# A sparse causal attention and a gated layer on one core: the sign mask of the queries taken from PSUM by halves, the relu moved to GpSimd, and a new written order

## The chip, the core and the metric

One core of a Trainium2 chip. The metric is the time of one execution on the device in microseconds; lower is better. The kernel before takes 178.91 us (median of 3 runs, 178.85 to 181.53).

## What is computed

Four batches, eight heads, 768 positions, head dimension 64. The keys are cut into 24 chunks of 32. For each query an upper bound of its score with any key of a chunk is computed from the chunk's minimum and maximum; the six best causal chunks are kept, and softmax attention runs over these alone. A gated layer follows.

```python
k_min, k_max = k_chunks.min(axis=3), k_chunks.max(axis=3)
ub = sum over d of maximum(q * k_min, q * k_max)
ub = where(causal, ub, -1e9); top_chunks = argsort(ub)[..., -6:]
scores = where(selected and causal, q @ k.T / 8, -1e9)
x = softmax(scores) @ v                       # heads side by side: 768 x 512
gate = sigmoid(causal convolution over 5 positions of x, per channel)
out = (gate * (x @ w_val)) @ w_out
```

Since max(q*min, q*max) = relu(q)*(max - min) + q*min, the bound is a matrix product of relu(q) and of q with two small key matrices. As the choice of six chunks needs more than fp16 gives, queries and keys are split into a high part and a low rest, both fp16: QH and QL of the queries, and for their positive part RH and RL.

## The kernel before

The work is done by pairs of heads: 16 pairs, four to a batch. All of a pair's steps are named in `build` with the pair's number behind the name:

- `Lk`, `Lq`, `Lv` load keys, queries and values (SP's queue). `KT` and `QT` turn keys and queries on TensorE into two PSUM banks each (L663), one for the head in either half (0 and 1).
- `KE` (L677, ScalarE) copies the turned keys to fp16. `KX` (L688, VectorE) takes maximum and minimum of each chunk; `KB` and `KS` (L696 to L713, GpSimd) make the small key matrices KB from them.
- `QH` (L717, ScalarE) writes the high part of the queries from PSUM, a half at a time. `QL` (L757, VectorE) takes the low rest, again from PSUM by halves. `RH` (L764, VectorE) is the maximum of QH and zero, `RM` (L770, VectorE) is QH > 0 as 0 or 1; each is one operation over 640 columns that reads and writes fp16 in SBUF. `RL` (L776, GpSimd) is QL times RM. Pair 0 does the same in fp32 (`KF`, `QF`, `RF`, `BF`).
- `CF` and `BD` (L743, L802, TensorE) add up the bounds from RH, RL, QH and QL with KB; `T8` (L810, VectorE) finds the eight largest and `CM` (L817) marks the chunks below the sixth. The marks are turned into a mask QM by TensorE and VectorE (`MT`, `ME`, L831) or by a DMA (`MD`).
- `S` (L845 to L850, TensorE) are six scores a pair, each for two heads, with the penalty added by a second product with the constant EM; `E` (L854, ScalarE) takes the exponentials; `A` (L866, GpSimd) sets the part above the diagonal to zero; `VC` (L786, GpSimd) casts the values; `AV` (L875, TensorE) multiplies; `RC` and `NR` (L881, L895, VectorE) divide by the sums.
- Per batch: the convolution for two of the pairs as products with diagonal matrices (`CV`, L950; the matrices `dg`, L1122, GpSimd) and for the other two as `CA` (L958) and four `CD` each (L963, VectorE); `TH` (tanh, ScalarE), `VL` (L976, L981, TensorE), `GV` (L986, VectorE), `OU` (L994, TensorE), `OE` (L1002 ScalarE, L1004 VectorE) and the store `ST`. The weights are loaded through GpSimd's queue (`wval`, `wnat`, `wout`).

Every operation of every engine stands in one long list of names, `ORDER`, written out in the file. `emit_in_order` issues the operations exactly in that order and gives PSUM banks (eight) out as the list comes to them, so that the list sets the order on each engine's queue and who gets which bank when. A bank is free again once the last operation that reads it has been issued; the next writer waits for that reader on the chip. The costs in `build` are those of the program that once made the list, and are not used when the kernel is built. RH, RL and RM have two buffers each, for even and odd pairs. `F` and `G` are 48 products with zeros that occupy TensorE during the start.

Of the kernel before, what the change touches and what calls it, by code (L numbers as in the profile page):

```python
# [1164 lines left out]
```

## Time and profile before

| | |
|---|---|
| median of 3 runs | 178.91 us (178.85 to 181.53) |
| profiled execution, its own time | 181.09 us |
| its span, first to last instruction | 179.3 us |
| busy: TensorE, VectorE, ScalarE, GpSimd | 167.9, 151.4, 151.3, 109.4 us |
| granted TensorE clock | 0.999 |
| data moved by DMA | 28.76 MB |

The profile is one execution. Busy time of TensorE is the union of its products, which overlap; a waiting engine shows as idle time in front of an instruction, with the instruction that released it behind an arrow. Row names are the tile written, the tiles read and the line. A row of the stretches gives the start and end of a stretch, its length, and the busy time of PE (TensorE), PEld (its weight loads), DVE (VectorE), ACT (ScalarE) and POOL (GpSimd) in it.

### The profile page before, as it was taken

To read this page: it belongs to the slowest core of one execution; us is meant where nothing else is said; L and a number is where in the kernel's file an instruction comes from. 1 tells how busy PE (TensorE), PEld (TensorE's weight loads), DVE (VectorE), ACT (ScalarE), POOL (GpSimd) and SP (SyncE) were. 2 spreads that over 40 slices of the span, in tenths; PEclk is the share of its full clock that TensorE was granted. 3 is DMA by queue.
4 is the path that set the end of the run, shared out by engine and by line. 5 is a ranking of instruction groups with operands and counts; after the bars stand their busy time and mean duration, and the time that the engine had idled before them with its cause. 6 is when DMAs were issued, how large, how long until landed. Compare 5 with 4: busy or idle time off the path is not lost.

```text
span 179.3 us, 7859 instructions
## 1 busy us (share of the span) xinstructions
PE 167.9 (94%) x3214; PEld 113.6 (63%) x3214; DVE 151.4 (84%) x456; ACT 151.3 (84%) x328; POOL 109.4 (61%) x231
## 2 busy tenths in 40 slices
PE   7999789999999999999999999977999999999991
PEld 5787557675676856667756587454855756685540
DVE  0599989984999999999999999986797899569960
ACT  3378899999999999799999998957699999979241
POOL 5758788999797998158829349687228913610000
PEclk9999999999999999999999999999999999999999
DMA  4999989984993999805990556927295370240955
GB/s 92 240 266 207 256 201 252 214 197 93 214 208 53 206 196 239 191 4 119 294 232 8 110 113 97 277 51 126 38 251 164 65 149 0 47 179 4 346 217 197
DMA packets 87315, 28.76 MB, mean 160 GB/s; under 512 B 82923, under 2 KB 84203, under 8 KB 87280
## 3 DMA queue, kind: packets, MB, share of 16 engines
q1 hardware_dynamic: 86192, 27.21, 63.2%
q0 software_dynamic: 1088, 1.06, 3.9%
q8 instruction: 25, 0.41, 1.0%
q14 instruction: 10, 0.08, 0.2%
HBM read 20.98 MB, written 6.29 MB: 152 GB/s over the span
## 4 chain that ended last, share of the span: by engine, by line
PE 60%; ACT 14%; DVE 10%; DMA 5%; POOL 5%; issue 4%; SPq 1%; ACTq 0%; POOLq 0%; DVEq 0%
PE ps L994 8%; ACT P L854 8%; PE ps L875 8%; PE ps L847 7%; PE ps L981 6%; PE ps L850 5%; PE ps L976 5%; PE ps L950 4%; PE ps L663 4%; PE ps L802 4%; DMA wn<-in_moe_w_val_dram 3%; DVE KK L688 3%; DVE QL L757 2%; ACT QH L717 2%; PE ps L1012 2%
## 5 line engine op out<-in xcount | busy, mean ns | idle before, releaser
L854 ACT ACTIVATE P<-ps 128x512 f16<-128x512 f32 (+1 forms) x192 | 91.5, 581 | 5.8 <-PE ps L875 2.7
L850 PE MATMUL ps<-QM,EM 64*128 64x512 f16 (+4 forms) x256 | 37.6, 290 | 0.7 <-DVE QM L831 0.7
L847 PE MATMUL ps<-QH,KE 64*128 64x512 f16 (+4 forms) x256 | 35.7, 292 | 1.7 <-DVE QL L757 1.6
L688 DVE TENSOR_REDUCE KK<-ps 128x12 f32<-128x384 f32 x64 | 32.0, 545 | 5.8 <-PE ps L655 4.8
L866 POOL TENSOR_SCALAR_AFFINE_SELECT P<-P 128x256 f16<-128x256 f16 (+1 forms) x64 | 32.6, 529 | 5.5 <-ACT P L854 3.8
L963 DVE SCALAR_TENSOR_TENSOR G<-ps,cwT,G 128x764 f32<-128x764 f16 (+3 forms) x32 | 32.1, 1006 | 2.6 <-ACT G L958 2.3
L776 POOL TENSOR_TENSOR RL<-QL,RM 128x640 f16<-128x640 f16 x15 | 21.1, 1409 | 12.1 <-DVE RM L770 10.9
L875 PE MATMUL ps<-VA,P 128*128 128x65 f16 x672 | 27.8, 194 | 0.1
L875 PEld LDWEIGHTS <-P 128*128 128x128 f16 x672 | 24.0, 98 | 4.9 <-issue 2.1
L994 PE MATMUL ps<-wo,GV 128*128 128x512 f16 (+1 forms) x100 | 22.7, 371 | 0.0
L847 PEld LDWEIGHTS <-KE 64*128 64x128 f16 x256 | 13.8, 94 | 9.5 <-issue 2.5
L677 ACT ACTIVATE KE<-ps 128x384 f16<-128x384 f32 x32 | 15.7, 537 | 4.5 <-PE ps L655 2.9
L895 DVE TENSOR_TENSOR ON<-ps,RCP 128x384 f16<-128x384 f32 x32 | 17.3, 552 | 0.6
L786 POOL CAST VA<-vn 128x768 f16<-128x768 f32 x16 | 13.8, 865 | 6.5 <-DMA vn<-in_v_dram 6.3
L757 DVE SCALAR_TENSOR_TENSOR QL<-ps,QH 128x320 f16<-128x320 f32 x30 | 14.0, 483 | 4.1 <-ACT QH L717 3.3
L986 DVE SCALAR_TENSOR_TENSOR GV<-G,ps 128x384 f16<-128x384 f32 x32 | 16.0, 547 | 1.4 <-PE ps L981 0.9
L810 DVE MAX8 TOP<-ps 128x8 f32<-128x12 f32 (+4 forms) x160 | 15.9, 163 | 1.2 <-PE ps L802 1.0
L1002 ACT ACTIVATE OSB<-ps 128x512 f32<-128x512 f32 (+1 forms) x22 | 13.3, 626 | 4.0 <-PE ps L994 4.0
L717 ACT ACTIVATE QH<-ps 128x384 f16<-128x384 f32 x32 | 14.9, 519 | 1.3 <-PE ps L663 1.2
L994 PEld LDWEIGHTS <-GV 128*128 128x128 f16 x100 | 9.0, 97 | 9.2 <-issue 0.6
L850 PEld LDWEIGHTS <-EM 64*128 64x128 f16 x256 | 12.4, 95 | 3.0 <-issue 1.7
L802 PE MATMUL ps<-KB,RH 128*128 128x48 f16 x150 | 13.0, 184 | 1.3 <-DVE TOP L810 1.0
(88 smaller groups left out, 328.9 us busy)
## 6 DMA issues: line engine op xcount, KB each, us to landing
vn<-in_v_dram SPq DMA_DIRECT2D x16, 384.0 KB, 5.1
out_dram<-OSB SPq DMA_DIRECT2D x23, 256.0 KB, 2.6
kn<-in_k_dram SPq DMA_DIRECT2D x30, 192.0 KB, 3.8
qn<-in_q_dram SPq DMA_DIRECT2D x30, 192.0 KB, 4.1
wo<-in_moe_w_out_dram POOLq DMA_DIRECT2D x4, 128.0 KB, 4.8
kn<-in_k_dram SPq DMA_DIRECT2D x4, 96.0 KB, 2.6
qn<-in_q_dram SPq DMA_DIRECT2D x4, 96.0 KB, 2.8
wv<-in_moe_w_val_dram POOLq DMA_DIRECT2D x4, 64.0 KB, 3.3
```

The costliest lines, as they stand in the source:

```text
L688: nc.vector.tensor_reduce(out=o, in_=i, axis=AX.X, op=ALU.min if mx else ALU.max)
L717: nc.scalar.activation(out=spread(QH[p % 3], p, w), in_=bank(gr, None), func=AF.Copy, scale=QS)
L757: nc.vector.scalar_tensor_tensor(out=spread(QL[p % 2], p, w), in0=bank(gr, None)[:, 1:NT], scalar=QS, in1=spread(QH[p % 3], p, w)[:, 1:NT] ...
L776: nc.gpsimd.tensor_tensor(out=RL[p % 2], in0=QL[p % 2], in1=RM[p % 2], op=ALU.mult)
L802: nc.tensor.matmul(out=o, lhsT=lt, rhs=kb[:, j, :], start=False, stop=(n == 5), skip_group_check=True)
L847: nc.tensor.matmul(out=pq[hh][:, col + a:col + n], lhsT=KE[p % 3][HP[hh], ks], rhs=QH[p % 3][HP[hh], q0 + a:q0 + n], start=True, stop=False)
L850: nc.tensor.matmul(out=pq[hh][:, col + a:col + n], lhsT=EM[HP[hh], ks], rhs=qm[HP[hh], q0 + a - 128:q0 + n - 128], start=False, stop=True)
L854: e.EX = lambda p, hh, bi, tot, gr: nc.scalar.activation(out=PT[bi, p % 2][:, hh, 0:tot], in_=bank(gr, None)[:, 0:tot], func=AF.Exp, scale ...
L866: nc.gpsimd.affine_select(out=ap, in_=ap, pattern=[[0, 2], [0, n], [1, 128]], compare_op=ALU.is_ge, fill=0.0, base=0, channel_multiplier=-1)
L875: nc.tensor.matmul(out=pav[:, qt, :], lhsT=PT[bi, p % 2][:, a, col:col + 128], rhs=VA[p % 3][:, hh, jt, :], start=(jt == 0), stop=(jt == qt))
L963: nc.vector.scalar_tensor_tensor(out=GT[sl][:, d:S], in0=bank(gr, None)[:, 0:S - d], scalar=cwT[:, NG + p % 2, n:n + 1], in1=GT[sl][:, d:S ...
L994: nc.tensor.matmul(out=po[:, 0:z - a], lhsT=GVT[(b % 2) * NCT + et][:, s * 128:(s + 1) * 128], rhs=wout_sb[:, et, a:z], start=(et == 0), s ...
```

## The change

Three things. RM is taken from the fp32 queries in PSUM instead of from QH in SBUF, by halves (two operations of 128x320 a pair instead of one of 128x640), like QL. RH is no longer a maximum on VectorE but the product of QH and RM on GpSimd, like RL. And the list of names is another one.

```diff
@@ build, queries
             n = SELT * 64
             c, l = dve(n)
-            if w:
-                g.op("DVE", 231, 320, f"RH{p}", lambda: e.RHv(p), [("QH", k3, w) for w in range(2)],
-                     [("RH", k2, w) for w in range(2)], ())
+            g.op("DVE", c, l, f"RM{p}.{w}", lambda w=w, gr=gr: e.RMv(p, w, gr), [("qps", p, w)],
+                 [("RM", k2, w)], [gr])
             g.op("DVE", c, l, f"QL{p}.{w}", lambda w=w, gr=gr: e.QLv(p, w, gr),
                  [("qps", p, w), ("QH", k3, w)], [("QL", k2, w)], [gr])
             if w:
-                g.op("DVE", 231, 320, f"RM{p}", lambda: e.RMv(p), [("QH", k3, w) for w in range(2)],
-                     [("RM", k2)], ())
+                g.op("POOL", 1350, 1396, f"RH{p}", lambda: e.RHv(p),
+                     [("RM", k2, w) for w in range(2)] + [("QH", k3, w) for w in range(2)],
+                     [("RH", k2, w) for w in range(2)], ())
                 g.op("POOL", 1350, 1396, f"RL{p}", lambda: e.RLv(p),
-                     [("RM", k2)] + [("QL", k2, w) for w in range(2)],
+                     [(x, k2, w) for x in ("RM", "QL") for w in range(2)],
                      [("RL", k2, w) for w in range(2)], ())
...
     def RHv(p):
-        nc.vector.tensor_scalar(out=RH[p % 2], in0=QH[p % 3][:, 128:S], scalar1=0.0, scalar2=None,
-                                op0=ALU.max)
+        nc.gpsimd.tensor_tensor(out=RH[p % 2], in0=QH[p % 3][:, 128:S], in1=RM[p % 2], op=ALU.mult)
-    def RMv(p):
-        nc.vector.tensor_scalar(out=RM[p % 2], in0=QH[p % 3][:, 128:S], scalar1=0.0, scalar2=None,
-                                op0=ALU.is_gt)
+    def RMv(p, w, gr):
+        nc.vector.tensor_scalar(out=spread(RM[p % 2], p, w), in0=bank(gr, None)[:, 1:NT],
+                                scalar1=0.0, scalar2=None, op0=ALU.is_gt)
```

The first and the last names of the list, before and after:

```diff
-mfz cwl F0 F1 F2 F3 F4 F5 Lk0.1 F6 F7 F8 F9 F10 F11 F12 mNS0 F13 F14 ident F15 KT0.1 cwn0 cwn1
-identb aw Lk0.0 KT0.0 mKB1 identh KE0.1
+Lk0.0 mfz cwl ident identh Lk0.1 Lk2.0 mKF0 F0 mNS1 F1 F2 F3 F4 F5 F6 F7 F8 aw mVA1 F9 F10 F11 F12
+F13 F14 F15 KT0.0 KX0.00 KX0.01 KT0.1 KX0.11 KE0.1 KX0.10
...
-OU3.2 OE3.2 ST3.2 OU3.1 OE3.1 ST3.1 OU3.0 OE3.0 ST3.0 OU3.5 OE3.5 ST3.5
+ST3.5z ST3.1 OU3.0 OE3.0 ST3.0 OU3.2 OE3.2 ST3.2
```

Three places of the new order. In the rows, ps is a PSUM tile; a buffer's number is that of its place in the ring (RM_107 belongs to even pairs, RM_108 to odd ones). Lines of the new kernel stand one or two higher.

*First*, VectorE right after QM of pair 0, with the first scores ahead. Before:

```order
L831 COPY QM_91<-ps_395 128x640
L757 SCALAR_TENSOR_TENSOR QL_102<-ps_403,QH_99 128x5x64
L770 TENSOR_SCALAR RM_108<-QH_99 128x640
L757 SCALAR_TENSOR_TENSOR QL_102<-ps_404,QH_99 128x5x64
L764 TENSOR_SCALAR RH_104<-QH_99 128x640
L764 TENSOR_SCALAR RH_103<-QH_100 128x640
L688 TENSOR_REDUCE KK_112<-ps_461 128x6x2
L688 TENSOR_REDUCE KK_112<-ps_460 128x6x2
L770 TENSOR_SCALAR RM_107<-QH_100 128x640
```

and after:

```order
L832 COPY QM_91<-ps_397 128x640
L759 SCALAR_TENSOR_TENSOR QL_102<-ps_358,QH_99 128x5x64
L759 SCALAR_TENSOR_TENSOR QL_102<-ps_359,QH_99 128x5x64
L771 TENSOR_SCALAR RM_107<-ps_403 128x5x64
L771 TENSOR_SCALAR RM_107<-ps_404 128x5x64
L759 SCALAR_TENSOR_TENSOR QL_101<-ps_403,QH_100 128x5x64
L759 SCALAR_TENSOR_TENSOR QL_101<-ps_404,QH_100 128x5x64
L690 TENSOR_REDUCE KK_112<-ps_465 128x6x2
```

The two relus are gone from here, and RM and QL of pair 2 stand in four halves ahead of the key maxima of pair 3; RM of pair 1 has moved ahead of QM, where QL of pair 2 stood.

*Second*, VectorE around the queries of pairs 12 to 14, with the key maxima of pair 14 between them. Before:

```order
L770 TENSOR_SCALAR RM_108<-QH_99 128x640
L688 TENSOR_REDUCE KK_111<-ps_3380 128x6x2
L688 TENSOR_REDUCE KK_111<-ps_3379 128x6x2
...
L764 TENSOR_SCALAR RH_103<-QH_98 128x640
L764 TENSOR_SCALAR RH_104<-QH_99 128x640
...
L810 MAX TOP_119<-ps_3429 128x8 x10
L817 TENSOR_TENSOR NS_121<-ps_3429,TOP_119 128x10x24
L764 TENSOR_SCALAR RH_103<-QH_100 128x640
L757 SCALAR_TENSOR_TENSOR QL_101<-ps_3641,QH_100 128x5x64
```

and after:

```order
L771 TENSOR_SCALAR RM_108<-ps_3368 128x5x64
L771 TENSOR_SCALAR RM_108<-ps_3369 128x5x64
...
L690 TENSOR_REDUCE KK_111<-ps_3414 128x6x2
L690 TENSOR_REDUCE KK_111<-ps_3413 128x6x2
...
L811 MAX TOP_119<-ps_3455 128x8 x10
L818 TENSOR_TENSOR NS_121<-ps_3455,TOP_119 128x10x24
L771 TENSOR_SCALAR RM_107<-ps_3442 128x5x64
L771 TENSOR_SCALAR RM_107<-ps_3441 128x5x64
L759 SCALAR_TENSOR_TENSOR QL_101<-ps_3441,QH_100 128x5x64
L759 SCALAR_TENSOR_TENSOR QL_101<-ps_3442,QH_100 128x5x64
```

The three relus have left the queue; two RM halves stand ahead of each pair's QL.

*Third*, GpSimd from the last load of `wval` to the key matrix of pair 7. Before:

```order
L1085 DMA wv_66<-in_moe_w_val_dram 32x2x512
L866 AFFINE_SELECT P_0_124<-P_0_124 128x4x128
L866 AFFINE_SELECT P_0_127<-P_0_127 128x2x128
L776 TENSOR_TENSOR RL_106<-QL_102,RM_108 128x640
L700 TENSOR_SCALAR KC_116<-KK_112 128x48
L713 TENSOR_TENSOR KC_116<-KQ_114,KC_116 128x48
L708 COPY KB_118<-KC_116 64x4x24 x2
```

and after:

```order
L1086 DMA wv_66<-in_moe_w_val_dram 32x2x512
L777 TENSOR_TENSOR RL_105<-QL_101,RM_107 128x640
L766 TENSOR_TENSOR RH_103<-QH_98,RM_107 128x640
L867 AFFINE_SELECT P_0_126<-P_0_126 128x2x256
L867 AFFINE_SELECT P_1_132<-P_1_132 128x2x256
L1092 DMA wn_67<-in_moe_w_val_dram 128x512
L713 TENSOR_SCALAR KQ_114<-KK_112 128x48
L766 TENSOR_TENSOR RH_104<-QH_99,RM_108 128x640
L702 TENSOR_SCALAR KC_116<-KK_112 128x48
L715 TENSOR_TENSOR KC_116<-KQ_114,KC_116 128x48
L710 COPY KB_118<-KC_116 64x4x24 x2
L777 TENSOR_TENSOR RL_106<-QL_102,RM_108 128x640
```

Four products over 640 columns, RL and RH of pairs 6 and 7, now stand between these two points, where one stood, the RL of pair 7.

More of the change, by code (lines that the diff above doesn't have):

```diff
@@ L205 @@
[L205 to L207 removed]
+Lk0.0 mfz cwl ident identh Lk0.1 Lk2.0 mKF0 F0 mNS1 F1 F2 F3 F4 F5 F6 F7 F8 aw mVA1 F9 F10 F11 F12
+F13 F14 F15 KT0.0 KX0.00 KX0.01 KT0.1 KX0.11 KE0.1 KX0.10 G0 mKB1 G1 G2 cwn1 KE0.0 identb KF0.01
+KF0.00 cwn0 cwt cws G3 G4 G5 G6 G7 KT2 KE2.1 KF0.10 KF0.11 KX2.11 KX2.01 G8 G9 G10 G11 G12 cfill
@@ new lines @@
+VC6 AV6.01 E7.12 Lq13.0 A6.4 AV6.02 AV6.12 T88.1 AV6.03 AV6.11 QH10.0 KE10.0 OE0.2 T88.4 T88.5
+T88.3 AV6.13 CM8 MT8 AV6.10 OU0.0 KE10.1 RM10.0 AV6.14 ME8 OE0.1 QL10.0 KX10.11 KX10.10 OE0.0
+AV6.15 S8.5 Lv10 E8.15 RC6.1 NR6.1 S8.1 E8.11 AV6.05 E8.05 AV6.00 AV6.04 RC6.0 E8.01 XT4 XTE4 S8.3
+E8.03 RH9 E8.13 KB9.0 NR6.0 KT11 S8.0 E8.00 S8.4 E8.04 E8.14 KB9.1 KS9 KX11.01 KB9.2 KB9.3 KX11.11
+CF9 KX11.00 RL9 KB9.4 BD9.1 BD9.4 BD9.3 KX11.10 BD9.2 BD9.5 E8.10 S8.2 KE11.1 QT11 A7.3 VC7 A7.1
+RL10 AV7.11 A7.4 AV7.14 T89.3 AV7.13 QH11.1 T89.2 AV7.04 AV7.12 T89.5 AV7.10 T89.4 T89.1 CM9 MT9
@@ new lines @@
+AV9.01 E10.04 AV9.02 E10.00 KX13.10 AV9.05 RC9.0 VL1.3 KX13.11 NR9.0 QT12 RM12.1 KE13.1 VL1.3z
+GV1.30 GV1.31 QH12.0 MD11 S11.5 QH12.1 RM12.0 E11.05 S11.3 E11.03 AV9.13 AV9.15 E11.15 RH12 QL12.1
+AV9.14 AV9.11 E11.13 QL12.0 Lv15 RL12 AV9.10 AV9.12 RC9.1 S11.1 E11.01 A10.1 S11.0 E11.10 KB12.2
+XT8 KB12.3 NR9.1 QT13 RM13.0 E11.11 VL1.2 RM13.1 KB13.0 S11.4 QH13.0 QL13.0 VL1.2z QH13.1 QL13.1
+E11.00 XT9 GV1.21 KT14 KX14.11 KX14.01 KB12.4 E11.14 E11.04 S11.2 E11.02 KX14.10 GV1.20 QT14 CF12
+KE14.0 KX14.00 E11.12 BD12.1 BD12.2 BD12.3 BD12.5 BD12.4 KE14.1 T812.3 QH14.1 OU1.5 OE1.5 T812.1
@@ new lines @@
+T812.4 T812.5 T812.2 CM12 XH9 CV9.0 A10.3 RL13 A11.4 CV9.1 TH9.00 TH9.11 A11.3 TH9.01 OU1.0 OE1.0
+TH9.10 A10.4 OU1.1 OE1.1 ST0.0 MD12 S12.5 S12.4 RM14.1 RM14.0 ST1.5 QH14.0 QL14.0 AV10.05 Lv12
+E12.05 AV10.04 QL14.1 AV10.03 AV10.02 E12.04 AV10.15 E12.15 AV10.13 AV10.10 AV10.11 AV10.12 AV10.14
+E12.14 Lq15.0 AV10.01 KB14.0 AV10.00 RC10.1 S12.1 E12.11 A11.1 KT15 RC10.0 NR10.0 NR10.1 S12.0
+E12.01 S12.2 S12.3 Lv14 KS13 KB13.1 KX15.01 KX15.10 E12.10 KX15.11 KB13.2 KB13.4 E12.00 E12.03 CF13
+RH13 KE15.1 KB13.3 BD13.1 BD13.4 BD13.3 A12.5 BD13.2 BD13.5 E12.02 XT10 KX15.00 T813.3 T813.1
@@ new lines @@
+AV11.01 T813.5 T813.4 AV11.04 AV11.02 AV11.00 KS14 AV11.03 CA10 A11.5 AV11.05 T813.2 CM13 QT15
+QH15.1 KB14.1 RC11.0 NR11.0 KB14.2 KB14.3 KB14.4 CD10.0 KE15.0 E12.13 QH15.0 OU1.2 OE1.2 RL14 A12.4
+QL15.1 OU1.4 ST1.1 OE1.4 CF14 RH14 BD14.3 BD14.2 E12.12 BD14.1 BD14.5 CD10.1 XTE10 MD13 RM15.1
+AV11.15 AV11.12 AV11.13 AV11.10 AV11.14 AV11.11 RC11.1 NR11.1 BD14.4 S13.4 E13.04 QL15.0 S13.1
+E13.01 E13.11 RM15.0 OU1.3 OE1.3 T814.4 T814.1 A12.1 VC12 T814.3 T814.2 T814.5 CM14 A12.3 AV12.03
+AV12.04 XT11 RL15 XTE11 E13.14 S13.3 CD10.2 E13.13 E13.03 ST0.5 CA11 CD10.3 VL2.0 VL2.0z GV2.01
@@ new lines @@
+AV12.13 AV12.00 AV12.05 AV12.02 AV12.01 RC12.0 GV2.00 ST1.0 AV12.10 AV12.14 AV12.15 S13.5 E13.15
+E13.05 NR12.0 S13.0 E13.00 E13.10 MD14 CD11.0 S14.2 S14.5 E14.05 AV12.11 AV12.12 RC12.1 KB15.0
+KB15.1 CF15 KS15 KB15.2 KB15.3 NR12.1 KB15.4 RH15 BD15.3 BD15.2 BD15.5 BD15.4 A13.5 A13.3 BD15.1
+S13.2 T815.1 E14.12 E14.15 VL2.1 VC15 Lv13 VC13 E14.02 S14.1 T815.5 T815.2 T815.4 T815.3 CM15 MD15
+E13.12 VL2.1z A14.5 CD11.1 A13.1 S14.4 E13.02 E14.11 S14.0 GV2.10 E14.01 VC14 GV2.11 E14.04 E14.14
+A14.4 VL2.2 S14.3 ST1.2 E14.10 VL2.2z CD11.2 CD11.3 E14.00 A13.4 AV13.14 AV13.02 TH10 AV13.15
@@ L238 @@
 PX = True
+RV = 2
 NPAIR = B * H // 2
```

161 lines of the change are left out of this document (65 added, 96 removed).

## The prediction

> **What bounds the kernel now.** I read the page's totals first, then the busy time by stretches, then single instructions of the two lines that change, then TensorE's own gaps.
>
> ```profile
> PE 167.9 (94%) x3214; PEld 113.6 (63%) x3214; DVE 151.4 (84%) x456; ACT 151.3 (84%) x328; POOL 109.4 (61%) x231
> ```
>
> TensorE is busy 94% of the span. The stretches say where the others stand beside it (start and end, length, then busy us of PE, PEld, DVE, ACT and POOL). Their borders are the first scores of pairs 0, 3, 6, 10, 13 and 15, found in the timeline by the 64x128 product that each pair has once, in the score listed first or nearly so.
>
> ```profile
> 0.00:16.00 16.00, 14.59 (x140) 11.62 (x141) 9.57 (x36) 8.38 (x21) 10.69 (x31) 1.00 0.93 209
> 16.00:37.20 21.20, 19.34 (x392) 13.95 (x393) 19.58 (x77) 20.32 (x48) 17.89 (x36) 1.00 0.99 224
> 37.20:63.00 25.80, 24.69 (x610) 17.53 (x608) 22.47 (x76) 25.24 (x59) 22.80 (x47) 1.00 0.73 157
> 63.00:105.60 42.60, 42.18 (x844) 27.98 (x845) 41.70 (x119) 40.38 (x86) 26.15 (x56) 1.00 0.72 157
> 105.60:130.70 25.10, 22.68 (x534) 15.78 (x534) 21.38 (x70) 19.98 (x48) 17.08 (x36) 1.00 0.54 114
> 130.70:151.90 21.20, 20.96 (x330) 12.69 (x330) 18.95 (x52) 20.65 (x43) 11.42 (x21) 1.00 0.52 124
> 151.90:170.00 18.10, 18.10 (x355) 11.36 (x355) 14.09 (x26) 13.60 (x26) 3.43 (x8) 1.00 0.39 135
> 170.00:179.30 9.30, 5.38 (x29) 2.64 (x27) 3.66 (x7) 2.77 (x5) 0.00 (x0) 0.98 0.59 215
> ```
>
> No single engine bounds it all. From 63 to 105.6 VectorE is busy 98% and TensorE 99%; from 37.2 to 63 ScalarE 98%, with GpSimd at 88%. TensorE idles 1.86, 1.11, 0.42, 2.42 and 0.24 us in the five stretches from 16.0 to 151.9, 6.05 us in all: that is what a better order can win there. GpSimd has room only after 63.
>
> **What the changed lines cost now.** First the groups (busy total, mean ns), then minimum, median and maximum of the same two lines.
>
> ```profile
> L764 DVE TENSOR_SCALAR RH<-QH 128x640 f16<-128x640 f16 x15 | 9.0, 613 | 2.5 <-ACT QH L717 2.5
> L770 DVE TENSOR_SCALAR RM<-QH 128x640 f16<-128x640 f16 x15 | 6.5, 434 | 0.0
> L764 DVE TENSOR_SCALAR RH<-QH x15: 301/321/1977, 17.3 to 141.7; 128x640 f16<-128x640 f16 x15
> L770 DVE TENSOR_SCALAR RM<-QH x15: 286/319/1117, 16.6 to 139.0; 128x640 f16<-128x640 f16 x15
> ```
>
> Median and mean lie far apart: most take 0.32 us, a few take up to 1.98. By the medians they would sum to 15 x 0.321 + 15 x 0.319 = 9.6 us; they sum to 15.5. Some 5.9 us are spent in a few long ones. The timeline shows what runs beside those:
>
> ```profile
> 17.32 1.74 DVE L764 TENSOR_SCALAR RH<-QH 128x640 f16<-128x640 f16 x2
> 17.48 1.40 POOL L776 TENSOR_TENSOR RL<-QL,RM 128x640 f16<-128x640 f16 x1
> 116.61 1.99 DVE L764 TENSOR_SCALAR RH<-QH 128x640 f16<-128x640 f16 x2
> 117.03 1.39 POOL L776 TENSOR_TENSOR RL<-QL,RM 128x640 f16<-128x640 f16 x1
> 122.85 1.98 DVE L764 TENSOR_SCALAR RH<-QH 128x640 f16<-128x640 f16 x1 [2.53 <-ACT QH L717]
> 122.86 1.01 POOL L866 TENSOR_SCALAR_AFFINE_SELECT P<-P 128x256 f16<-128x256 f16 x2
> 123.83 0.82 POOL L786 CAST VA<-vn 128x768 f16<-128x768 f32 x1
> 124.75 0.48 DVE L757 SCALAR_TENSOR_TENSOR QL<-ps,QH 128x320 f16<-128x320 f32 x1
> ```
>
> Each long one ends when a run of GpSimd's work ends: at 122.85 the relu sits out two masks and a cast (until 124.65), and QL starts at 124.75. So these SBUF-to-SBUF forms wait for GpSimd, while QL, which reads PSUM, never took over 0.49 us in 30 times:
>
> ```profile
> L757 DVE SCALAR_TENSOR_TENSOR QL<-ps,QH x30: 462/482/492, 14.7 to 138.6; 128x320 f16<-128x320 f32 x30
> ```
>
> The Trainium skill states this in SBUF — State Buffer, Who interferes with whom: a copy or tensor_scalar that uses both SBUF ports of VectorE, and a GpSimd instruction, hold a shared port pair one at a time and for their whole length, whereas one with at most one SBUF input outside those modes does not compete. The trace agrees (1.98 us against a median of 0.321; QL's maximum 0.492).
>
> Do the long ones reach TensorE? Its three largest inner gaps:
>
> ```profile
> 21.09 0.21 PE L802 MATMUL ps<-KB,RH 128*128 128x48 f16 x2 [1.02 <-DVE TOP L810]
> 119.12 1.20 PE L950 MATMUL ps<-xT,diag 32*32 32x384 f16 x82 [0.94 <-DVE KK L688]
> 125.28 0.39 PE L847 MATMUL ps<-QH,KE 64*128 64x512 f16 x1 [1.14 <-DVE QL L757]
> ```
>
> Each comes shortly after one of the three long stalls and is released by what stands behind it on VectorE: 1.02 + 0.94 + 1.14 = 3.1 us.
>
> **The change part by part.** *1. The stalls go.* The compare now reads PSUM, like QL, and the relu leaves VectorE. At the three places I count VectorE's own time. A half-size operation out of PSUM is priced at 0.42 us (part 2). Around 17.32 (first pair of order fences) six of them now stand where two QL halves, two RM and the two relus stood: 2.5 us against 0.84 + 0.64 + 1.74 = 3.2, so -0.7. Around 116.61 (second pair) two relus of 1.99 together and two RM at the median 0.32 make 2.6 us; four halves take 1.7, so -0.9. At 122.85 one relu of 1.98 and its RM of 0.32 make 2.3; two halves take 0.85, so -1.4. Together -3.0, nearly the three gaps. Bounds: 0, if something else releases TensorE just then, to -3.1. I take -3.0, since all three chains run over VectorE.
>
> *2. What is new on VectorE.* No row shows a compare out of PSUM. Nearest: QL of the same shape, and the output scaling, a tensor_scalar out of PSUM (0.424 us for 256 columns, 0.690 for 512: 0.49 by interpolation for 320). In a row QL takes 1.69 / 4 = 0.42 each, and two undisturbed relus 0.55:
>
> ```profile
> 111.71 1.69 DVE L757 SCALAR_TENSOR_TENSOR QL<-ps,QH 128x320 f16<-128x320 f32 x4
> 76.70 0.55 DVE L764 TENSOR_SCALAR RH<-QH 128x640 f16<-128x640 f16 x2
> L1004 DVE TENSOR_SCALAR OSB<-ps x3: 424/690/690, 172.0 to 175.4; 128x512 f32<-128x512 f32 x2, 128x256 f32<-128x256 f32 x1
> ```
>
> A pair so pays 0.85 instead of 0.55: +0.3, 4.5 us over 15 pairs, against 5.9 us of stalls. In sum VectorE loses 1.4 us, but not where it is full: from 37.2 to 105.6 the new order lists twelve halves, six pairs' worth, 5.1 us, where six pairs took 3.3 and RM's one stall there (1.117, so 0.8) makes it 4.1: +0.95 or so. That I charge whole, because VectorE is at 94 to 98% there; bounds 0 (TensorE covers it) to 1.8 (no stall was on the path).
>
> The Trainium skill, VectorE: DVE Perf Modes, Why PSUM operands drop a tier, says that an fp32 operand in PSUM limits VectorE to one element a cycle. QL's 0.48 us fits that; its rule speaks against the change in these six pairs, and the sum by it is the same +0.95.
>
> *3. GpSimd.* It gets 15 products of the size of RL, 21.1 us, and goes from 109.4 to 130.5.
>
> ```profile
> L776 POOL TENSOR_TENSOR RL<-QL,RM 128x640 f16<-128x640 f16 x15 | 21.1, 1409 | 12.1 <-DVE RM L770 10.9 <-PE ps L850 0.8
> L866 POOL TENSOR_SCALAR_AFFINE_SELECT P<-P 128x256 f16<-128x256 f16 (+1 forms) x64 | 32.6, 529 | 5.5 <-ACT P L854 3.8 <-issue 1.2
> L786 POOL CAST VA<-vn 128x768 f16<-128x768 f32 x16 | 13.8, 865 | 6.5 <-DMA vn<-in_v_dram 6.3
> L708 POOL COPY KB<-KC 64x96 f16<-64x96 f16 x30 | 8.0, 267 | 1.5
> L1122 POOL TENSOR_TENSOR diag<-ident,cw 128x320 f16<-128x320 f16 x4 | 2.8, 718 | 0.0
> ```
>
> From the first score of pair 3 to that of pair 10 the new order lists on GpSimd 8 RH more, 3 casts, 2 masks, 1 diagonal and 4 small KB steps more: 11.3 + 2.6 + 1.1 + 0.7 + 1.1 = 16.8 us on top of 48.95 in 68.4 us, so 65.7, 96%. Pairs 3 to 5 alone: 22.80 + 3 x 1.41 + 0.87 + 0.72 - 1.41 (one RL fewer) = 27.2 us where the stretch lasted 25.8. Behind such a product in the queue stand the masks that the attention products wait for, and KB, RL and RH of the next pair, for which its block products wait (third pair of order fences). Price: from 0 (GpSimd lags a little and recovers after 63, where it has 16 us free) to 1.4, and to 4.4 if its 3.0 us of waits in that stretch stay. I take half of 1.4, 0.7.
>
> *4. Start.* The first key maxima waited until 5.99 although three transposes were done at 5.14, because the half loaded second was listed first:
>
> ```profile
> 4.50 0.64 PE L655 MATMUL ps<-ident,kn 128*128 128x128 f32 x3
> 5.99 1.95 DVE L688 TENSOR_REDUCE KK<-ps 128x12 f32<-128x384 f32 x4 [4.83 <-PE ps L655]
> ```
>
> The new order loads, turns and reduces half 0 first: 0 to -0.85; ScalarE and the second key load follow anyway, so -0.4. The first mask copy still has two half-size operations ahead of it, RM now, QL before.
>
> *5. End.* The last block is now a whole one (256 KB, by ScalarE) instead of a half (128 KB, by VectorE):
>
> ```profile
> 174.99 0.60 ACT L1002 ACTIVATE OSB<-ps 128x512 f32<-128x512 f32 x1 [1.08 <-PE ps L994]
> 175.42 0.42 DVE L1004 TENSOR_SCALAR OSB<-ps 128x256 f32<-128x256 f32 x1 [0.61 <-PE ps L994]
> out_dram<-OSB SPq DMA_DIRECT2D x23, 256.0 KB, 2.6
> out_dram<-OSB SPq DMA_DIRECT2D x2, 128.0 KB, 2.0
> ```
>
> Now the whole block of 174.99 lands about 175.6 + 2.6, the half 175.8 + 2.0. Ending on a whole one at 176.0 + 2.6 costs 0.4 to 0.8 (0.18 + 0.6): +0.5.
>
> *Sum:* -3.0 + 0.95 + 0.7 - 0.4 + 0.5 = -1.25 us. The profiled execution took 181.09 us (span 179.3, 1.8 around it), 2.2 above the median of 178.91; so 179.8 for its like and **177.7 us** for the median, 0.7% faster. What a measurement here can tell from no change is about 2%, 3.6 us.
>
> **Rivals.** *A, faster:* TensorE is the only bound, so the 0.95 and the 0.7 lie hidden, the stalls go, and the shorter VectorE queue takes half of the remaining 6.05 - 3.1 us of inner gaps too: -3.0 - 1.5 - 0.4 + 0.5 = -4.4, 174.5 us. For it: TensorE's 99 to 100% in the later stretches. Against: VectorE's 98% from 63 to 105.6.
>
> *B, slower:* GpSimd becomes what the block products wait for. It decides where GpSimd's list exceeds the stretch (27.2 against 25.8 us in pairs 3 to 5) and its waits of 3.0 us do not shrink: +4.4. Then RH comes late from GpSimd instead of from VectorE (RM, then two products of 1.41 us, 2.8 us, where 1.41 was), and the three gaps stay: 0 + 0.95 + 4.4 - 0.4 + 0.5 = +5.45, 184.4 us. For it: the 96%. Against: casts and small steps can run ahead. The Trainium skill points the same way: GPSIMD Engine Reference, Engine selection, advises against two-input elementwise work on GpSimd, calling it about twice as slow as on VectorE; here 1.41 us stand against VectorE's 0.32, which is worse still.
>
> *C, the change does not do what it says:* the compare out of PSUM is held up beside GpSimd as well. Then no stall goes, and the full +1.8 and the 0.7 are paid: +1.8 + 0.7 - 0.4 + 0.5 = +2.6, 181.5 us. Against: QL's maximum of 0.492 in 30 runs.
>
> **How the numbers follow.** Forecast 0.50, of which 0.02 reaches beyond 2% on the fast side; A 0.22; B 0.18; C 0.10, within 2%. So faster 0.24, within 2% 0.58, slower 0.18. The forecast's own spread from the bounds is some 175.5 to 180.5. The range of 173.8 to 183.2 takes in A and C and most of the way to B, and leaves out about 0.2.
>
> **What would show it.** Right: every RM half at 0.46 to 0.50 us, none over 0.6; RH on GpSimd at 1.4; GpSimd's total near 130 and VectorE's near 150; TensorE's gaps behind VectorE in stretches like 114 to 126 gone. B: gaps of TensorE released by RH or RL, and AV products waiting for masks, between the first scores of pairs 3 and 10. A: TensorE's idle time between first and last score under 3 us. Wrong in my steps: VectorE's idle time growing, because RM now holds the query banks and transposes wait for them; or a start that is later than before.

## Result and profile after

The changed kernel takes 181.91 us (median of 20 runs, 180.68 to 183.01); before, over the runs made beside them, takes 180.91 (178.85 to 181.71). The ratio is 1.0118, with a 95% interval of 1.0086 to 1.0150: slower, by less than the 2% that count as a difference. I had forecast 0.7% faster. The median of three runs that stood ahead of the prediction, 178.91 us, was 2.0 below that; the profiled execution of before (181.09) was not.

Most runs of before lie between 180 and 182.5 us and a few between 177.8 and 179.1, and the ratios weigh these few more than the medians do; so where two of my own kernels are compared below, I use their medians in us (beside them, the median of before lay between 180.83 and 181.02). By medians the change costs +1.0 us, by the ratio about 2.

The profiled execution of the changed kernel took 183.01 us (span 181.3), the longest of its 20 runs, 1.1 above their median and 1.9 above the profiled one of before. The page's totals first:

```profile
PE 168.2 (93%) x3214; PEld 114.0 (63%) x3214; DVE 152.0 (84%) x456; ACT 151.4 (84%) x328; POOL 129.0 (71%) x246
```

TensorE's work is the same (167.9 before). Its idle time, span minus busy, went from 11.4 to 13.1 us. VectorE gained nothing in sum; GpSimd got 19.6 us more. Next the stretches (start and end, length, busy us of PE, PEld, DVE, ACT, POOL), cut as before, at the first scores of pairs 0, 3, 6 and 10 and near those of 13 and 15:

```profile
0.00:17.00 17.00, 14.78 (x140) 11.72 (x141) 11.06 (x37) 8.02 (x21) 11.68 (x37) 1.00 0.93 211
17.00:37.60 20.60, 19.78 (x391) 13.54 (x392) 19.16 (x72) 20.43 (x50) 19.90 (x30) 1.00 0.86 194
37.60:64.20 26.60, 24.14 (x585) 17.14 (x582) 23.74 (x79) 24.81 (x58) 25.37 (x47) 1.00 0.77 153
64.20:106.40 42.20, 40.77 (x805) 27.45 (x805) 40.54 (x116) 38.43 (x81) 36.30 (x68) 1.00 0.82 175
106.40:130.00 23.60, 22.62 (x528) 15.31 (x528) 18.75 (x63) 21.09 (x49) 15.73 (x31) 1.00 0.59 120
130.00:152.00 22.00, 21.22 (x389) 14.38 (x387) 20.29 (x64) 21.16 (x44) 16.44 (x29) 1.00 0.67 120
170.00:181.30 11.30, 6.90 (x36) 3.33 (x34) 4.71 (x10) 3.80 (x7) 0.00 (x0) 0.94 0.51 186
```

TensorE's idle time (length minus PE) in each stretch, and its change:

| stretch | before | after | change |
|---|---|---|---|
| start | 1.41 | 2.22 | +0.81 |
| 17.0 to 37.6 | 1.86 | 0.82 | -1.04 |
| 37.6 to 64.2 | 1.11 | 2.46 | +1.35 |
| 64.2 to 106.4 | 0.42 | 1.43 | +1.01 |
| 106.4 to 130 | 2.42 | 0.98 | -1.44 |
| 130 to 152 | 0.24 | 0.78 | +0.54 |
| end | 3.92 | 4.40 | +0.48 |

The two stretches with the three stalls win 2.5 us, the two from 37.6 to 106.4 lose 2.4, and the start loses 0.8. GpSimd is busy 25.37 of 26.6 us from 37.6 to 64.2, 95%, and 36.30 of 42.2 from 64.2 to 106.4, 86%, where it was 61%. It is just as full ahead of these, 19.90 of 20.6 us from 17.0 to 37.6, 97%; the gain there is the gap that the first stall had made. TensorE's block products (L803) now wait for what GpSimd wrote, which none of them did before. These are TensorE's gaps of 0.4 us or more from 6 to 170, with their releasers:

```profile
12.72 1.51 PE L753 MATMUL ps<-KF,QF 128*128 128x48 f32 x12 [1.00 <-DVE NS L818]
50.60 0.21 PE L803 MATMUL ps<-KB,RH 128*128 128x48 f16 x2 [0.86 <-POOL KB L710]
53.33 0.44 PE L828 MATMUL ps<-identh,NS 128*128 128x128 f16 x5 [0.60 <-ACT P L855]
64.85 0.23 PE L851 MATMUL ps<-QM,EM 64*128 64x128 f16 x2 [0.42 <-DVE QM L832]
67.66 0.20 PE L803 MATMUL ps<-KB,RL 128*128 128x48 f16 x1 [0.93 <-POOL RL L777]
114.24 0.23 PE L851 MATMUL ps<-QM,EM 64*128 64x128 f16 x2 [0.54 <-DMA QM<-NS]
126.47 0.23 PE L851 MATMUL ps<-QM,EM 64*128 64x128 f16 x2 [0.44 <-DMA QM<-NS]
143.72 0.39 PE L851 MATMUL ps<-QM,EM 64*128 64x512 f16 x2 [0.65 <-DMA QM<-NS]
```

The gap at 67.66 ends at the third place of the order that was shown ahead. GpSimd's own timeline there:

```profile
62.91 0.33 POOL L713 TENSOR_SCALAR KQ<-KK 128x48 f32<-128x48 f32 x1
63.32 1.40 POOL L766 TENSOR_TENSOR RH<-QH,RM 128x640 f16<-128x640 f16 x1
64.80 0.33 POOL L702 TENSOR_SCALAR KC<-KK 128x48 f16<-128x48 f32 x1
65.22 0.28 POOL L715 TENSOR_TENSOR KC<-KQ,KC 128x48 f16<-128x48 f32 x1
65.56 0.57 POOL L710 COPY KB<-KC 64x96 f16<-64x96 f16 x2
66.20 1.40 POOL L777 TENSOR_TENSOR RL<-QL,RM 128x640 f16<-128x640 f16 x1
```

It does not pause; the new RH stands ahead of the key matrix and of RL, RL ends at 67.60, and the block products start 0.06 us later. In the chain that ended last, GpSimd's share rose from 5% to 26%:

```profile
PE 48%; POOL 26%; ACT 11%; DMA 6%; DVE 4%; issue 3%; POOLq 0%; ACTq 0%; DVEq 0%
```

Nearly all of it lies in three long runs of GpSimd's work, from 14.6 to 22.2 us, 23.3 to 50.6 and 56.8 to 67.6, between which TensorE or ScalarE carry the chain. The first of them ends like this (start, length, what):

```profile
16.69 1.39 POOL RH L766
18.09 1.36 POOL RL L777
19.45 1.35 POOL RH L766
20.80 1.36 POOL RL L777
22.21 0.42 PE ps L803 x10
```

The changed operations took what I had priced them at (minimum, median, maximum of the two lines):

```profile
L766 POOL TENSOR_TENSOR RH<-QH,RM x15: 1392/1399/1412, 16.7 to 141.8; 128x640 f16<-128x640 f16 x15
L771 DVE TENSOR_SCALAR RM<-ps x30: 446/480/492, 15.2 to 137.7; 128x320 f16<-128x320 f32 x30
```

### The profile page after: what moved, and what is told of

It reads as the page before. It is cut to its first block, busy times and chain, and to the rows that moved or that the text cites. A ratio compares the mean times of both kernels' runs of the same rounds, so it can differ in the third digit from the quotient of the medians.

```text
span 181.3 us, 7871 instructions
## 1 busy us (share of the span) xinstructions
PE 168.2 (93%) x3214; PEld 114.0 (63%) x3214; DVE 152.0 (84%) x456; ACT 151.4 (84%) x328; POOL 129.0 (71%) x246
## 4 chain that ended last, share of the span: by engine, by line
PE 48%; POOL 26%; ACT 11%; DMA 6%; DVE 4%; issue 3%; POOLq 0%; ACTq 0%; DVEq 0%
PE ps L995 8%; PE ps L876 7%; DMA QM<-NS 6%; POOL RL L777 6%; POOL RH L766 6%; ACT P L855 5%; PE ps L982 5%; PE ps L977 5%; PE ps L848 4%; PE ps L851 4%; POOL P L867 4%; PE ps L803 4%; PE ps L1013 3%; DVE KK L690 3%; PE ps L665 2%
## 5 line engine op out<-in xcount | busy, mean ns | idle before, releaser
L867 POOL TENSOR_SCALAR_AFFINE_SELECT P<-P 128x512 f16<-128x512 f16 (+1 forms) x64 | 32.9, 530 | 9.0 <-ACT P L855 7.1
L848 PE MATMUL ps<-QH,KE 64*128 64x512 f16 (+4 forms) x256 | 36.4, 291 | 0.5
L876 PE MATMUL ps<-VA,P 128*128 128x65 f16 x672 | 27.3, 194 | 0.2 <-ACT P L855 0.2
L766 POOL TENSOR_TENSOR RH<-QH,RM 128x640 f16<-128x640 f16 x15 | 21.0, 1399 | 4.8 <-DVE RM L771 4.3
L679 ACT ACTIVATE KE<-ps 128x384 f16<-128x384 f32 x32 | 16.3, 536 | 7.4 <-DVE KK L690 7.4
L719 ACT ACTIVATE QH<-ps 128x384 f16<-128x384 f32 x32 | 16.4, 552 | 0.7 <-PE ps L665 0.4
L851 PEld LDWEIGHTS <-EM 64*128 64x128 f16 x256 | 12.3, 94 | 6.6 <-issue 5.3
L1003 ACT ACTIVATE OSB<-ps 128x512 f32<-128x512 f32 (+1 forms) x22 | 12.8, 610 | 4.3 <-PE ps L995 4.3
L771 DVE TENSOR_SCALAR RM<-ps 128x320 f16<-128x320 f32 x30 | 14.0, 479 | 1.7 <-ACT QH L719 1.1
```

The source lines that it names most:

```text
L719: nc.scalar.activation(out=spread(QH[p % 3], p, w), in_=bank(gr, None), func=AF.Copy, scale=QS)
L766: nc.gpsimd.tensor_tensor(out=RH[p % 2], in0=QH[p % 3][:, 128:S], in1=RM[p % 2], op=ALU.mult)
L848: nc.tensor.matmul(out=pq[hh][:, col + a:col + n], lhsT=KE[p % 3][HP[hh], ks], rhs=QH[p % 3][HP[hh], q0 + a:q0 + n], start=True, stop=False)
L851: nc.tensor.matmul(out=pq[hh][:, col + a:col + n], lhsT=EM[HP[hh], ks], rhs=qm[HP[hh], q0 + a - 128:q0 + n - 128], start=False, stop=True)
L867: nc.gpsimd.affine_select(out=ap, in_=ap, pattern=[[0, 2], [0, n], [1, 128]], compare_op=ALU.is_ge, fill=0.0, base=0, channel_multiplier=-1)
L876: nc.tensor.matmul(out=pav[:, qt, :], lhsT=PT[bi, p % 2][:, a, col:col + 128], rhs=VA[p % 3][:, hh, jt, :], start=(jt == 0), stop=(jt == qt))
```

## Experiments

Theory 1: GpSimd's 15 new products make what stands behind them late, and this eats what VectorE gains. Theory 2: the new list itself costs the time, whatever the operations. Busy time and idle time below are those of each profiled execution, the time is the median, and the ratio is to before.

| kernel | GpSimd busy | TensorE idle | us | ratio, 95% interval |
|---|---|---|---|---|
| before | 109.4 | 11.4 | 180.9 | |
| after | 129.0 | 13.1 | 181.91 | 1.0118, 1.0086 to 1.0150 |
| old_order_new_ops | 128.6 | 17.1 | 189.62 | 1.0483, 1.0455 to 1.0511 |
| new_order_old_ops | 109.6 | 22.3 | 194.98 | none |
| new_rh_short | 112.0 | 9.8 | 179.01 | 0.9885, 0.9851 to 0.9918 |
| new_rh_short_early | 118.5 | 10.3 | 179.50 | 0.9913, 0.9882 to 0.9944 |
| new_rh_short_late | 121.8 | 11.5 | 180.97 | 0.9999, 0.9976 to 1.0023 |
| new_vc_short | 119.0 | 9.3 | 179.35 | 1.0015, 0.9967 to 1.0064 |
| new_rh_max | 135.4 | 16.4 | 185.76 | 1.0333, 1.0264 to 1.0402 |
| new_rm_short | 128.9 | 12.3 | 181.69 | 1.0097, 1.0052 to 1.0142 |
| new_half_last | 129.0 | 12.2 | 181.62 | 1.0083, 1.0047 to 1.0118 |
| old_relus_later | 109.9 | 8.7 | 177.64 | 0.9871, 0.9795 to 0.9948 |
| old_new_ops_12_14 | 113.8 | 9.6 | 179.72 | 0.9952, 0.9926 to 0.9978 |

### The two halves crossed

old_order_new_ops keeps before's list and puts the new operations where the old ones stood:

```diff
-... QL2.0 ... QL2.1 ... RL2 ...       (RM2 and RH2 elsewhere on VectorE)
+... RM2.0 QL2.0 ... RM2.1 QL2.1 ... RH2 RL2 ...
```

> The new operations in the order of before: the two halves of RM stand right ahead of the two halves of QL, and RH on GpSimd right ahead of RL; all else keeps its place. Theory 1 (GpSimd: the second product of 1.40 us a pair delays KB, RL and the masks, whatever the list): slower than before, by 1 to 4 us, ratio 1.005 to 1.02, with TensorE gaps released by RL, RH or KB from 37 to 106 us. Theory 2 (the operations are neutral or better, and the new list is the worse one, by its start, its end and its late masks): faster than before by 1 to 3 us, ratio 0.985 to 0.995, since the stalls of RH and RM are gone.

new_order_old_ops keeps the new list and puts the old operations into it:

```diff
-... RM2.0 ... RM2.1 ... RH2 ...       (RM halves on VectorE, RH on GpSimd)
+... RM2 (at the later half's place) ... RH2 ...       (both on VectorE)
```

> The old operations in the new order: RM as one operation out of SBUF where the later of its halves stood, RH as a maximum on VectorE where it stood on GpSimd. Theory 1: GpSimd is relieved of 21 us, so faster than the changed kernel by 1 to 3 us, ratio to before 0.995 to 1.005; the stalls of RH and RM come back at some places and take up to 2 us of that. Theory 2: as slow as the changed kernel or slower, ratio 1.01 to 1.03.

Both came out far worse than either theory had said: 189.62 and 194.98 us (the latter from 191.56 to 196.99). The gaps say why. In the first, RH stands right ahead of RL in GpSimd's queue, and TensorE waits for what comes behind the two:

```profile
20.75 0.20 PE L802 MATMUL ps<-KB,RL 128*128 128x48 f16 x1 [0.99 <-POOL RL L776]
29.53 0.20 PE L802 MATMUL ps<-KB,RL 128*128 128x48 f16 x1 [1.05 <-POOL RL L776]
39.31 0.21 PE L802 MATMUL ps<-KB,RH 128*128 128x48 f16 x2 [1.06 <-POOL KB L709]
```

In the second, RH is written by VectorE at a place in the list that was meant for GpSimd, and TensorE waits for VectorE:

```profile
30.19 0.22 PE L801 MATMUL ps<-KB,RH 128*128 128x48 f16 x2 [1.61 <-DVE RH L763]
41.23 0.22 PE L801 MATMUL ps<-KB,RH 128*128 128x48 f16 x2 [1.39 <-DVE RH L763]
```

So list and operations belong together, and a crossing does not price either by itself. The first agrees with theory 1 in kind and goes against theory 2, which had it faster than before; the second goes against theory 1, which had it faster than the changed kernel. Together they do not tell the theories apart. I went on within the new list, changing only how long an operation takes.

### GpSimd's load within the new list

new_rh_short leaves out 608 of the 640 columns of each RH product (the rest of RH stays zero); list and waits are those of the changed kernel:

```diff
-nc.gpsimd.tensor_tensor(out=RH[p % 2], in0=QH[p % 3][:, 128:S], in1=RM[p % 2], op=ALU.mult)
+nc.gpsimd.tensor_tensor(out=RH[p % 2][:, 0:32], in0=QH[p % 3][:, 128:160],
+                        in1=RM[p % 2][:, 0:32], op=ALU.mult)
```

> The changed kernel with the product RH on GpSimd over 32 columns of 640 only, the rest left at zero, so that the choice of chunks is another one (two memsets of VectorE at the start besides, while it idles). All waits, places and buffers stay. Theory 1: some 1.2 us less a pair on GpSimd, 18 us in all; faster than the changed kernel by 1.5 to 3 us, ratio to before 0.995 to 1.003. Theory 2: no more than 0.5 us faster than the changed kernel, ratio 1.009 or more.

The group row of RH, then TensorE's only three gaps of 0.3 us or more between 17 and 172, then the shares of the chain that ended last:

```profile
L766 POOL TENSOR_TENSOR RH<-QH,RM 128x32 f16<-128x32 f16 x15 | 3.7, 247 | 4.4 <-DVE RM L772 4.0
```

```profile
51.77 0.44 PE L829 MATMUL ps<-identh,NS 128*128 128x128 f16 x5 [0.82 <-ACT P L856]
63.04 0.23 PE L852 MATMUL ps<-QM,EM 64*128 64x128 f16 x2 [0.42 <-DVE QM L833]
139.66 0.39 PE L852 MATMUL ps<-QM,EM 64*128 64x512 f16 x2 [0.47 <-DMA QM<-NS]
```

```profile
PE 65%; ACT 21%; DMA 6%; DVE 3%; issue 2%; ACTq 0%; DVEq 0%
```

None of the three is released by GpSimd, and GpSimd has left the chain altogether. 179.01 us, 2.9 below the changed kernel and 1.9 below before: the length of the RH products is worth 2.9 us, which is theory 1. This does not price the list by itself: the three stalls are gone in this kernel as well, and old_relus_later below, which has the old list without them, is another 1.4 us faster.

new_vc_short takes 10.0 us off GpSimd (new_rh_short took 17.0) from another operation: it leaves out eleven twelfths of each cast of the values.

```diff
-nc.gpsimd.tensor_copy(out=o, in_=i)
+nc.gpsimd.tensor_copy(out=o[:, 0:1], in_=i[:, 0:1])
```

> The changed kernel with the casts of the values (VC) over one of twelve parts only, the rest of VA at zero, so that the output is another one (memsets of VectorE at the start, while it idles). RH and RL stay as they are; GpSimd loses some 0.65 us a pair elsewhere. Theory, occupation: a third to a half of the 2.9 us goes, ratio 0.999 to 1.007. Rival, the length of the way RM, RH, RL to the block products: less than 0.4 us, ratio 1.009 or more.

GpSimd 119.0 us, 179.35 us: 2.6 faster than the changed kernel, though RH itself is as long as there. By medians that is nine tenths of the 2.9, more than the third to half that I had expected, by the ratios under a half. Either way it is how full the queue is that costs, not only that RH comes late. The casts stand ahead of attention products as well; what shorter ones would win in before was not run.

new_rh_max takes RH as a maximum with zero on GpSimd, out of QH alone, so that it needs no RM:

```diff
-nc.gpsimd.tensor_tensor(out=RH[p % 2], in0=QH[p % 3][:, 128:S], in1=RM[p % 2], op=ALU.mult)
+nc.gpsimd.tensor_scalar(out=RH[p % 2], in0=QH[p % 3][:, 128:S], scalar1=0.0, scalar2=None,
+                        op0=ALU.max)
```

> The changed kernel with RH on GpSimd as a maximum of QH and zero (one tensor read) instead of a product with RM (two read); the result is the same. The cast of 768 columns took 0.86 us on GpSimd, so a maximum over 640 would take some 0.75 instead of 1.40. Theory: GpSimd's occupation is the cost (2.9 us for 1.4 us a pair), so about half of it goes: ratio to before 0.996 to 1.004. Rival: what costs is that RH waits for GpSimd's queue at all; then 1.008 or more. If the maximum takes 1.4 us too, nothing changes.

I had expected a shorter operation. It is longer, 1.81 us against the product's 1.40:

```profile
L766 POOL TENSOR_SCALAR RH<-QH x15: 1802/1811/1842, 16.4 to 145.0; 128x640 f16<-128x640 f16 x15
```

The size was a miss, but it made the test run the other way: 6.4 us more on GpSimd, 3.85 us more time, with more and longer gaps behind it:

```profile
30.79 0.20 PE L804 MATMUL ps<-KB,RL 128*128 128x48 f16 x1 [1.01 <-POOL RL L778]
70.40 0.20 PE L804 MATMUL ps<-KB,RL 128*128 128x48 f16 x1 [1.27 <-POOL RL L778]
138.32 0.22 PE L804 MATMUL ps<-KB,RH 128*128 128x48 f16 x2 [1.04 <-POOL RH L766]
```

Then where. new_rh_short_early has the short product (608 columns left out) for pairs 1 to 9 alone, new_rh_short_late for pairs 10 to 15 alone:

```diff
+n = 32 if p < 10 else S - 128          (late: 32 if p > 9)
-nc.gpsimd.tensor_tensor(out=RH[p % 2], in0=QH[p % 3][:, 128:S], in1=RM[p % 2], op=ALU.mult)
+nc.gpsimd.tensor_tensor(out=RH[p % 2][:, 0:n], in0=QH[p % 3][:, 128:128 + n],
+                        in1=RM[p % 2][:, 0:n], op=ALU.mult)
```

> The changed kernel with RH on GpSimd over 32 of 640 columns for pairs 1 to 9 only (the choice of chunks is another one there); pairs 10 to 15 keep the whole product. Theory: the cost of GpSimd's added work lies in the stretch where its list fills the time (37 to 106 us, pairs 3 to 9), so most of what the short product of all pairs won comes back: ratio to before 0.988 to 0.998. Rival, GpSimd costs as much per product late as early: 0.999 to 1.005.

> The same for pairs 10 to 15 only, pairs 1 to 9 whole. Theory: GpSimd has room there, so at most a third of the gain of all pairs (the scores that wait for late masks by DMA): ratio 1.003 to 1.012. Rival: 0.995 to 1.002.

Early: 179.50 us, 2.4 of the 2.9. Late: 180.97, 0.9 of them, the third that the theory allowed at most; but its ratio of 0.9999 missed the 1.003 to 1.012 of the theory and lies in the rival's 0.995 to 1.002. In the late kernel the gap behind RL of pair 7 stays as it was and those at 114 and 126 are gone; one behind a late mask remains:

```profile
67.17 0.20 PE L805 MATMUL ps<-KB,RL 128*128 128x48 f16 x1 [0.91 <-POOL RL L779]
141.86 0.39 PE L853 MATMUL ps<-QM,EM 64*128 64x512 f16 x2 [0.71 <-DMA QM<-NS]
```

GpSimd's share of the chain is 24% there and 7% in the early kernel, against 26% in the changed one.

So by medians the loss sits for four fifths in pairs 1 to 9 and for a third in the last six, by the ratios for nine tenths and a half; the two add to more than the whole. In the later pairs it takes another way: the changed kernel's chain runs over a late RL and RH (131.96 to 135.12) to the block products, the marks, and a mask sent by DMA that lands at 143.68. The gap near 140 to 144 stays with short products too (0.47, 0.71), so that one is not GpSimd's alone.

### VectorE, and the end

new_rm_short leaves out 256 of the 320 columns of each RM half, which takes 6.3 us off VectorE (I had expected 7.5):

```diff
-nc.vector.tensor_scalar(out=spread(RM[p % 2], p, w), in0=bank(gr, None)[:, 1:NT],
+nc.vector.tensor_scalar(out=spread(RM[p % 2], p, w)[:, 0:1], in0=bank(gr, None)[:, 1:2],
```

> The changed kernel with each half of RM over 64 of its 320 columns, the rest left at zero, so that the choice of chunks is another one. VectorE loses 0.25 us a half, 7.5 us in all; GpSimd keeps all its work. If VectorE is a bound beside GpSimd (my term of 0.95 us): 1 to 2 us faster than the changed kernel, ratio 1.001 to 1.007. If GpSimd alone holds TensorE up: ratio 1.009 or more.

181.69 us, 0.2 below the changed kernel: nothing that can be told apart. What VectorE's halves cost where GpSimd holds nothing up was not run. The gaps behind GpSimd stay:

```profile
49.60 0.21 PE L803 MATMUL ps<-KB,RH 128*128 128x48 f16 x2 [0.93 <-POOL KB L710]
66.65 0.20 PE L803 MATMUL ps<-KB,RL 128*128 128x48 f16 x1 [0.93 <-POOL RL L777]
```

new_half_last moves the block that is stored by halves back to the end of the list:

```diff
-... OU3.5 OE3.5 ... ST3.5 ... OU3.2 OE3.2 ST3.2
+... OU3.2 OE3.2 ST3.2 OU3.5 OE3.5 ST3.5
```

> The changed kernel with the half block of the last rows as the last block, as before. By the profiles the end lasts 3.9 us behind the last product before and 4.4 us after the change. Both theories: 0.4 to 0.6 us faster than the changed kernel, ratio to before 1.008 to 1.010. If the end does not matter: 1.012.

181.62 us, 0.3 lower, with intervals that overlap: the sign is the expected one, the size is not settled. Nor does its profile show a shorter end. TensorE idles 10.60 - 6.23 = 4.37 us there from 170 on, against 4.40 in the changed kernel and 3.92 before:

```profile
170.00:180.60 10.60, 6.23 (x33) 3.04 (x31) 4.13 (x9) 3.15 (x6) 0.00 (x0) 1.00 0.54 198
```

### The stalls by themselves

old_relus_later is before with its own operations; only the three relus of the long stalls stand later on VectorE's queue:

```diff
-... RH2 ... KX3.00 ... RH13 ... KX14.00 ... RH14 QL14.0 ... QL14.1 ...
+... KX3.00 RH2 ... KX14.00 RH13 ... QL14.0 ... QL14.1 RH14 ...
```

> The kernel before with three names moved in its list and nothing else: the relus of pairs 2, 13 and 14, which waited for GpSimd's lock in front of key maxima and QL, stand right behind these (RH2 behind KX3.00, RH13 behind KX14.00, RH14 behind QL14.1). If the three TensorE gaps of 3.1 us came from these stalls: 1.5 to 3 us faster than before, ratio 0.983 to 0.992. If something else would have held TensorE there: ratio 0.997 to 1.003.

177.64 us, 1.3% below before by the ratio (0.5 to 2.0%) and 1.8% by medians: it beats both kernels. The relus still wait for GpSimd, but at places where less stands behind them (maximum 1.161 us, 1.977 before):

```profile
L763 DVE TENSOR_SCALAR RH<-QH x15: 301/320/1161, 17.0 to 138.4; 128x640 f16<-128x640 f16 x15
```

TensorE's three gaps of 1.02, 0.94 and 1.14 are gone; after 41 us its largest two are behind loads:

```profile
113.12 0.58 PE L662 MATMUL ps<-ident,kn 64*128 64x64 f32 x12 [0.51 <-DMA kn<-in_k_dram]
133.18 0.59 PE L662 MATMUL ps<-ident,qn 64*128 64x64 f32 x12 [0.56 <-DMA qn<-in_q_dram]
```

old_new_ops_12_14 is before with the new operations in pairs 12 to 14 alone, where GpSimd has room:

```diff
+new = p in (12, 13, 14)
+if new: RM by halves out of PSUM ahead of each QL half, RH on GpSimd ahead of RL
```

> The kernel before, order and all, with the new operations in pairs 12, 13 and 14 alone (RM halves right ahead of QL's, RH on GpSimd right ahead of RL). There VectorE's relus waited for GpSimd, and GpSimd is busy 17 of 25 us. Theory: where GpSimd has room the change does what it says; the gaps of 0.94 and 1.14 us at 119 and 125 us go: 1 to 2 us faster than before, ratio 0.988 to 0.995. Rival, RH late on GpSimd takes the place of the stall: 0.998 to 1.006.

179.72 us, 1.3 below before by medians, 0.5% by the ratio, which is just short of the 0.988 to 0.995 that was expected and short of the rival's 0.998 as well. The gap at 125.28 is gone, the one near 119 too; the one near 21, which lies outside these pairs, stays (1.04); a new one of 0.60 stands at 114.53, where key transposes wait for a bank until a QL half has read it:

```profile
114.53 0.55 PE L671 MATMUL ps<-ident,kn 64*128 64x64 f32 x11 [0.60 <-DVE QL L765]
```

In these three pairs, where GpSimd has room, the change does what it says.

## Why the prediction was wrong, step by step

*1, the stalls go (-3.0): right.* No RM half took over 0.492 us, so rival C is out; that its 181.5 us is the nearest of all the forecasts to the 181.91 measured is chance. The two stretches with the stalls lost 2.5 us of TensorE's idle time; what is left from 106.4 to 130 is two waits for late masks (0.54 and 0.44). Removed by themselves in old_relus_later, the three stalls were worth 2.3 us by the ratio (0.9 to 3.7) and 3.3 by medians.

*2, VectorE (+0.95): too much.* Taking 6.3 us off VectorE changed the time by 0.2. That fits the lower bound I had named, 0; but it was measured in a kernel that GpSimd holds up, so the term is shown to be hidden there, not to be nothing.

*3, GpSimd (+0.7): the step that failed.* Its busy time was forecast well (130.5, measured 129.0), but not what it costs: 2.9 us by new_rh_short. "I take half of 1.4, 0.7" took the 1.4 us by which GpSimd's list exceeded the stretch of pairs 3 to 5 (27.2 against 25.8), as if that stretch alone were full and GpSimd recovered behind it. The occupation came out lower there, 25.37 of 26.6 us, and from 37.6 to 106.4 it was 61.67 of 68.8, 90%, where I had 96%. But it reaches further forward: from 17.0 to 37.6, which I did not price, GpSimd was busy 97%, and the chain runs over its queue from 14.6 to 67.6 with one longer break. Each pair's key matrix, RH and RL stand there behind the products of other pairs, and late ones stop TensorE more than once (0.86 at 50.60, 0.93 at 67.66). It is the mechanism of rival B, at two thirds of its price of 4.4; the other half of B, that the three gaps stay, did not happen. That the cost ends at 63 was wrong as well: by new_rh_short_late 0.9 us of it comes from pairs 10 to 15, over late RH and RL and the masks behind them.

*4, start (-0.4): did not show.* The key maxima came 0.6 us earlier:

```profile
5.39 1.49 DVE L690 TENSOR_REDUCE KK<-ps 128x12 f32<-128x384 f32 x3 [4.22 <-PE ps L657]
```

Yet the first score came 1.0 later (17.00 against 16.00), with a gap of 1.00 at 12.72 behind the marks. Ahead of these on VectorE, two operations on 20 columns of the convolution's weights took 0.85 us each, where each took 0.18 before:

```profile
8.12 0.85 DVE L1116 CAST cw<-cwT 128x20 f16<-128x20 f32 x1
9.01 0.85 DVE L1117 TENSOR_TENSOR cw<-cwT,cw 128x20 f16<-128x20 f32 x1
```

Each ended within 0.05 us of an operation of GpSimd's that ran beside it (8.93 and 9.81): these look like the stalls of part 1 again, at another place. In the profile of new_vc_short, whose list is the same, the first took 0.18 and the second 0.71, and the gap was 0.26. By the first score of pair 1 the two kernels stand level (23.15 and 23.20), but only because the first stall's gap of 1.02 is gone between; the start itself cost 0.8 in this execution.

*5, end (+0.5): agrees in the one profile,* +0.48 there, but the reason is not shown: with the half block last again the end idled as long (4.37). The last two scalings were on ScalarE, as in the forecast:

```profile
176.07 0.60 ACT L1003 ACTIVATE OSB<-ps 128x512 f32<-128x512 f32 x1 [1.29 <-PE ps L995]
176.98 0.60 ACT L1003 ACTIVATE OSB<-ps 128x512 f32<-128x512 f32 x1 [0.32 <-PE ps L995]
```

With what was measured the sum is -2.5 + 0.2 + 2.9 + 0.8 + 0.5 = +1.9 us, as between the two profiled executions; with the 3.3 of old_relus_later in place of 2.5 it is +1.1, near the +1.0 by medians. The parts come from different kernels and overlap (late masks are in the 2.5 as well as in the 2.9), so that it closes is not evidence for any of them. The level was off too: 177.7 us stood on a median of 178.91, where twenty runs gave 180.91; 1.25 below that would have been 179.7.

Rival A did not happen: TensorE's idle time rose. The Trainium skill, GPSIMD Engine Reference, Engine selection, had advised against this kind of product on GpSimd. The trace agrees in direction, 1.40 us for the product against 0.32 for VectorE's undisturbed maximum; as to the kernel's time, the products cost 2.9 us and the three stalls 2.3 to 3.3, so no run here shows which of the two is dearer.

Open: what the list costs or gains by itself, since both crossings broke the fit of list and operations; whether the gap near 143 belongs to the list; and what lengthens the end.

## What to carry to other kernels

An engine at 61% on average can be nearly full in some stretches; count what a moved operation adds in each of them, the early ones too, and look whether the engine's queue becomes the chain that ends last, rather than pricing the excess of one stretch. When an operation stalls in a few of its places only, moving those few in the queue (here 177.64 us) can be worth more than giving all of them to another engine (181.91). And a median of three runs may be low: compare the profiled execution's own time with it before placing a forecast.

## What the runs showed of the hardware

On GpSimd a maximum of one fp16 tensor with a constant over 640 columns took 1.81 us, longer than the product of two such tensors, 1.40 us; on VectorE an undisturbed maximum of the same size took 0.32. Two VectorE operations on 20 columns took 0.85 us each beside GpSimd's work, 0.18 elsewhere. GpSimd's load did not cost in proportion: within the new list, the 17.0 us from 112.0 to 129.0 cost 2.9 us, the 6.4 us from there to 135.4 cost 3.85.
